# A spectral mixing and SoLU kernel: the twiddle table loaded without gaps and in two parts, x read two chunks at a time, one weight piece converted later

## The chip, the cores and the metric

The kernel runs on one core of a Trainium2 chip. The metric is the time of one launch in microseconds (us), the median of several runs. The profile is one execution recorded by the hardware profiler; its times count from the first instruction. Engines are named as in the profile: PE is the matrix engine (PEld its weight loads), DVE the vector engine, ACT the scalar engine, POOL the GpSimd engine, SP the sync engine, which here does nothing but issue DMAs.

## The reference

```python
def reference(x, w_in, w_out, g_ln):            # x: 8 x 3136 x 256, float32
    X = np.fft.fft(np.fft.fft(x, axis=1), axis=2).real.astype(np.float32)
    t = X.reshape(25088, 256)
    h = t @ w_in                                # w_in: 256 x 1024
    e = np.exp(h - h.max(-1, keepdims=True))
    u = h * e / (e.sum(-1, keepdims=True) + 1e-9)
    u = (u - u.mean(-1, keepdims=True)) / np.sqrt(u.var(-1, keepdims=True) + 1e-6)
    return ((u * g_ln) @ w_out).astype(np.float32)   # w_out: 1024 x 256
```

The weights arrive as 64-bit floats. The kernel sees each of them as two 32-bit words and makes a 32-bit float of them itself.

## The kernel before

The transform over 3136 = 49 x 64 positions is done in two stages. The batch of 8 goes in four pairs. For a pair, 98 partitions hold 2 sequences x 49 values of n1, and the free dimension holds n2 and the 256 features. Since only the real part is wanted, position n2 is first added to its mirror (`add_mirror`, L124) and features d and 256-d are added and subtracted (`fold`, L132). The 32 remaining values of n2 go in eight chunks of four (`CH = 4`, so one chunk of one partition is 4 KB). `load` (L99) fetches a chunk: its own rows go to `xa` over SP's queue, the mirror rows go to `xb` by an indirect DMA that POOL issues. `transform1` (L143) multiplies a chunk by the table `F`, ACT copies the product to `z`, and `keep` (L176) stores it in a scratch tensor `zd` in HBM. `turn` (L179) reads five values of k1 (`KG = 5`) back from `zd` with n2 on the partitions, as `g`. `transform2` (L186) multiplies `g` by the twiddle table `T`, whose rows and columns are split by the two sequences of the pair: the blocks that mix two sequences are zero. `take2` (L198) copies the product to `q`, and `spread` (L202) sends one row of `q` to all partitions as `r`.

The feature transform is folded into the first weight matrix: `product_in` (L448) multiplies the table `Q` by the converted `w_in` and gives `Wi` and `w_mid`. Then come 100 units, one for each pair and each k1 from 0 to 24. A unit makes two blocks of 128 tokens (one if k1 is 0): `up` (L217) on PE, `even` and `join` (L225, L231) on DVE, `expo` on ACT, `product` on DVE with a small mean on POOL, `square` on ACT, `stats` on POOL. The block is then turned: units 0 to 3 by PE transposes (`turn_whole`, L293), all later ones by DVE block transposes and 16 DMAs on SP (`move_blocks`, L310). Four units later (`lag = 4`) `down` (L319) multiplies by `Wo` on PE, `scale` on ACT and `store` finish it. `centre` (L480) subtracts from `Wo` its mean over rows, once.

The order of instructions on each engine is the order in which the code emits them: nothing reorders them. A DMA issue waits on SP like any instruction, and what stands behind it on SP waits too. Semaphores of SP's DMAs are reused in turns of eight, so that an issue also waits until the one eight places earlier has landed.

What matters for the change is the start (L517 to L602), before and during the first units. SP's order is: the first pieces of `w_in` between chunks 0 and 1 of x and `F`; the own rows of chunks 2 and 3; `Q` and `g_ln`; chunks 4 and 5; chunks 6 and 7 and the small stores to `zd`; then, in the middle of chunk 3's step, the two halves of `w_out` (`load_out`) and the table `T` (`load_table`, L437). Chunks 2 to 5 lie in two buffers named `room` that later hold `raw_out` and `uT`. After the eighth chunk, `turn(first, 0, ...)` reads the first `g`, half over SP and half over POOL. The conversion of a weight piece is `exponent`, `confine` and `narrow` (L364 to L405); `narrow` takes the low word by a shift to the right by one and a multiplication by 2^-31. Four pieces of 512 words per partition make `w_in`, four more make `w_out` (`narrow_out(0)` to `narrow_out(3)`, L580 and L585), and all are converted before unit 0 begins. The other four `turn`s of the first pair are issued by POOL in units 0 to 3 (L645).

Of the kernel before, what the change touches and what calls it, by code (L numbers as in the profile page):

```python
# [8 lines left out]

FP32 = mybir.dt.float32  # L10
I32 = mybir.dt.int32
ALU = mybir.AluOpType
ACT = mybir.ActivationFunctionType
AX = mybir.AxisListType
# [20 lines left out]
def kernel(  # L35
# [27 lines left out]
    x_g = x.rearrange("b (n1 g l) d -> (b n1 g) (l d)", n1=N1, l=CH)  # L63
    x_pn = x.rearrange("b (n1 n2) d -> (b n1) n2 d", n2=N2)
    out_k = out.rearrange("(p k2 k1) d -> p k1 k2 d", p=NP, k1=N1)

# [9 lines left out]
    ps_m = ctx.enter_context(tc.tile_pool(name="ps_m", bufs=4, space=PSUM))  # L76

    F = const.tile([PR, 6, ZR], FP32, name="F")
    T = const.tile([P, NK, P], FP32, name="T")
    Wi = const.tile([P, KD, FF], FP32, name="Wi")  # L80
    Wo = const.tile([P, KF, D], FP32, name="Wo")
    ones = const.tile([P, P], FP32, name="ones")
    ident = const.tile([P, P], FP32, name="ident")
    neg_half = const.tile([P, 2], FP32, name="neg_half")
    idx = const.tile([P, NP * (NC + NK - 1)], I32, name="idx")
    w_mid = const.tile([P, FF], FP32, name="w_mid")
    g_ln = const.tile([P, KF], FP32, name="g_ln")
    wbar = const.tile([P, D], FP32, name="wbar")
# [7 lines left out]
            self.raw, self.y, self.y0 = {}, {}, None  # L96
            self.g, self.zs = {}, {}

    def load(pr, c, room=None):  # L99

        r = slice(pr.p * PR, (pr.p + 1) * PR)
        if room is None:
            xa = xpool.tile([PR, CH, D], FP32, tag="xa", name="xa")
            xb = xpool.tile([PR, CH, D], FP32, tag="xb", name="xb")
        else:
            xa, xb = (t.rearrange("p (l d) -> p l d", d=D) for t in room)
# [79 lines left out]
    def transform2(pr, k1):  # L186

        i, k = divmod(k1, KG)  # L190
        g = pr.g[i]
        ps = ps_m.tile([P, KD * P], FP32, tag="m", name="ps2")
        for h in range(KD):
            nc.tensor.matmul(ps[:, h * P : (h + 1) * P], g[:, k, h * P : (h + 1) * P], T[:, k1, :],  # L194
                             start=(h == 0), stop=True, skip_group_check=True)
        return ps

# [163 lines left out]
    def bits(o, i, a, op0, b=None, op1=ALU.bypass):  # L361
        nc.vector.tensor_scalar(out=o, in0=i, scalar1=a, scalar2=b, op0=op0, op1=op1)
# [23 lines left out]
    def narrow(w, raw, outs, unit):  # L386

        if w.dtype == FP32:
            for o, scale in outs:
                nc.vector.tensor_scalar(out=o, in0=o, scalar1=scale, scalar2=2.0 ** 20, op0=ALU.mult, op1=ALU.mult)  # L390
            return
        lo, hi = raw[:, 0 : 2 * NW : 2], raw[:, 1 : 2 * NW : 2]

        bits(mantissa, hi, 0xFFFFF, ALU.bitwise_and, 0x100000, ALU.bitwise_or)
        bits(lo, lo, 1, ALU.logical_shift_right)
        m = lo.bitcast(FP32)
        nc.vector.scalar_tensor_tensor(out=m, in0=lo, scalar=2.0 ** -31, in1=mantissa, op0=ALU.mult, op1=ALU.add)

        nc.vector.scalar_tensor_tensor(out=unit, in0=hi, scalar=top_bit, in1=unit, op0=ALU.bitwise_and,
                                       op1=ALU.bitwise_or)  # L400
        n = NW // len(outs)
        for i, (o, scale) in enumerate(outs):
            r = slice(i * n, (i + 1) * n)
            nc.vector.scalar_tensor_tensor(out=o, in0=m[:, r], scalar=scale, in1=unit[:, r].bitcast(FP32),
                                           op0=ALU.mult, op1=ALU.mult)  # L405

    class Weights:
# [26 lines left out]
            nc.sync.dma_start(out=self.Q, in_=q_tab.rearrange("(c p) d -> p c d", p=P))  # L434
            nc.sync.dma_start(out=g_ln, in_=moe_g_ln.rearrange("(c p) -> p c", p=P))

        def load_table(self):  # L437
            for b in range(2):
                r = slice(b * N2, (b + 1) * N2)
                nc.sync.dma_start(out=T[r, :, r], in_=t_tab)  # L440

        def mid(self):

# [73 lines left out]
    with tc.manual_schedule():  # L517
# [2 lines left out]
        nc.sync.dma_start(out=idx, in_=mirror)  # L520
        make_identity(nc, ident)

        rooms = {}
        for c in range(2, 6, 2):
            room = fpool.tile([P, 2, KF, 4, 64], FP32, tag="uT", name="room", bufs=2)
            room = room[0:PR].rearrange("p w c i m -> p (w c i m)").rearrange("p (a n) -> p a n", a=4)
            rooms[c], rooms[c + 1] = [room[:, i] for i in (0, 1)], [room[:, i] for i in (2, 3)]
        weights.load_in()
        for c in range(4):
            weights.piece_in(c)  # L530
            if c:
                load(first, c - 1, rooms.get(c - 1))
            if c == 1:
                nc.sync.dma_start(out=F, in_=f_tab)
        load(first, 3, rooms[3])
        weights.load_tables()
        for c in range(4, 6):
            load(first, c, rooms[c])
        nc.vector.memset(ones, 1.0)
        nc.vector.memset(neg_half, -0.5)  # L540
        bits(top_bit, neg_half[:, 0:1].bitcast(I32), 31, ALU.logical_shift_right, 31, ALU.logical_shift_left)
# [5 lines left out]
        for c in range(NC):  # L547
# [15 lines left out]
            if c == 3:  # L563
                weights.place_out()
                for i in range(2):
                    weights.load_out(i)
                weights.load_table()
                weights.mid()
                weights.scale_out()
            for s in range(CH // 2):  # L570
                transform1(first, c * CH // 2 + s)
            if c == 3:
                weights.product_in(0)
        turn(first, 0, (nc.sync, nc.gpsimd) * 2)

        confine(weights.units[0], True)
        for i in range(1, 3):
# [3 lines left out]
        weights.exponent_out(3)  # L581
        confine(weights.units[-1])
        weights.product_in(2)
        for i in range(1, 4):
            weights.narrow_out(i)  # L585

        units = [Unit(p, k1) for p in range(NP) for k1 in range(NK)]
# [7 lines left out]
        for i in range(len(units) + lag):  # L595
# [57 lines left out]
def _tables(B, S, D):  # L653
# [30 lines left out]
    mirror = np.zeros((P, B // 2 * (NC + NK - 1)), np.int32)  # L684
    mirror[:PR, : B // 2 * NC] = load.transpose(1, 0, 2).reshape(PR, -1)
    rows = np.arange(B)[:, None, None] * S + (N1 - np.arange(1, NK)) + N1 * np.arange(N2)[::-1, None]
    mirror[:, B // 2 * NC :] = rows.reshape(B // 2, P, NK - 1).transpose(1, 0, 2).reshape(P, -1)
# [39 lines left out]
```

## Time and profile before

| what | value |
|---|---|
| median of 3 runs | 1193.29 us (1191.67 to 1194.35) |
| profiled execution, span of the core | 1189.9 us |
| PE busy | 1154.2 us, 97% of the span |
| DVE busy | 907.9 us, 76% |
| ACT busy | 679.0 us, 57% |
| POOL busy | 496.9 us, 42% |

The span has four parts. Up to about 62 us, x, the tables and the weights come in and the first pair is transformed. From there to about 98 us the first units fill the pipeline. From 98 us to 1172 us the units repeat, and the last 18 us finish the last of them. In the lines that follow, an entry like `58.54 1.99 PE L194 ...` gives the start, the length, the engine, the line, the tiles and the number of instructions, and in square brackets the time the engine stood idle before and what ended that.

### The profile page before, as it was taken

Reading aid. Unit: us, or ns where it says so; the run is one execution under the profiler, and the core shown is the slowest. Engines: PE = TensorE matmul, PEld = TensorE weight load, DVE = VectorE, ACT = ScalarE, POOL = GpSimd, SP = SyncE. Lnnn points to the kernel's source line nnn. Section 1 sums busy time; section 2 is a strip of 40 time slices with the busy share of each in tenths; the row PEclk is TensorE's granted clock in tenths of the full one; section 3 lists DMA queues with packets and bytes.
Section 4 is the critical chain, followed back from the end, with each engine's and each line's share of the span. In section 5 each row is a group of like instructions: output and inputs, shape, how many; then the busy total and the mean of one; then the engine's idle time right before and its main releaser. Section 6 shows DMA issues by size and latency. Waiting matters only on the chain. (4 is left out here: it accounts for less than half of the span.)

```text
span 1189.9 us, 15918 instructions
## 1 busy us (share of the span) xinstructions
PE 1154.2 (97%) x4720; PEld 875.9 (74%) x4720; DVE 907.9 (76%) x1241; ACT 679.0 (57%) x1404; POOL 496.9 (42%) x964
## 2 busy tenths in 40 slices
PE   2889999999999999999999999999999999999998
PEld 1556777777777777777777777777777777777787
DVE  8879777777768877787778878777786887877780
ACT  4557655655546656565555656565555555655561
POOL 3045444443544443432544453433453344333433
PEclk9999999999999999999999999999999999999999
DMA  9873765756775765654775776664684453544534
GB/s 246 206 187 72 190 162 152 200 140 163 171 172 160 187 172 155 167 144 131 172 187 159 176 177 154 158 181 122 150 198 131 109 152 100 145 111 120 142 92 117
DMA packets 460886, 185.39 MB, mean 156 GB/s; under 512 B 428854, under 2 KB 442750, under 8 KB 460800
## 3 DMA queue, kind: packets, MB, share of 16 engines
q1 hardware_dynamic: 446848, 145.63, 48.6%
q0 software_dynamic: 13952, 38.75, 11.9%
q8 instruction: 38, 0.62, 0.2%
q14 instruction: 48, 0.39, 0.1%
HBM read 44.78 MB, written 38.80 MB: 70 GB/s over the span
## 5 line engine op out<-in xcount | busy, mean ns | idle before, releaser
L323 PE MATMUL ps_o<-Wo,uT 128*128 128x256 f32 x3136 | 693.4, 379 | 0.3 <-ACT ot L328 0.3
L323 PEld LDWEIGHTS ps_o<-Wo,uT 128*128 128x128 f32 x3136 | 611.0, 196 | 62.8 <-issue 0.9
L222 PE MATMUL ps_h<-Wi,q 128*128 128x512 f32 x800 | 362.3, 595 | 0.1
L254 DVE SCALAR_TENSOR_TENSOR u<-h,u 128x1024 f32<-128x1024 f32 x196 | 240.1, 1225 | 57.0 <-ACT u L246 31.1
L236 DVE CUSTOM_DVE_ANT_0 h<-ev,ps_h 128x1024 f32<-128x1024 f32 x196 | 231.8, 1219 | 50.3 <-PE ps_h L222 41.3
L256 POOL TENSOR_SCALAR nmean<-usum 128x1 f32<-128x1 f32 x196 | 80.4, 411 | 445.7 <-DVE u L254 445.5
L222 PEld LDWEIGHTS ps_h<-Wi,q 128*128 128x128 f32 x800 | 152.7, 191 | 149.8 <-issue 144.6
L263 ACT ACTIVATE h<-u,nmean 128x1024 f32<-128x1024 f32 x196 | 225.0, 1149 | 61.3 <-POOL nmean L256 60.0
L228 DVE SCALAR_TENSOR_TENSOR ev<-w_mid,r,ps_h 128x1024 f32<-128x1024 f32 x100 | 127.8, 1278 | 133.1 <-PE ps_h L222 126.2
L246 ACT ACTIVATE u<-h,neg 128x1024 f32<-128x1024 f32 x196 | 225.4, 1150 | 6.5
L291 DVE STREAM_TRANSPOSE v<-u 128x1024 f32<-128x1024 f32 x192 | 228.6, 1236 | 0.1
L200 ACT COPY q<-ps 128x256 f32<-128x256 f32 x100 | 37.2, 372 | 289.3 <-PE ps L194 263.0
L328 ACT ACTIVATE ot<-ps_o,rs 128x256 f32<-128x256 f32 x196 | 87.0, 462 | 61.3 <-PE ps_o L323 55.2
L335 POOL DMA_INDIRECT out_dram<-ot,idx x96 | 103.0, 1073 | 35.4 <-issue 20.7
L194 PEld LDWEIGHTS ps<-T,g 128*128 128x128 f32 x400 | 60.9, 194 | 52.1 <-issue 50.9
L169 PE MATMUL ps<-y,F 98*100 98x258 f32 (+3 forms) x288 | 72.2, 387 | 22.2 <-DVE y L122 22.2
L278 POOL TENSOR_TENSOR rs<-v,neg_half 128x2 f32<-128x2 f32 (+1 forms) x100 | 84.2, 842 | 7.8
L244 ACT ACTIVATE neg<-nmax 128x1 f32<-128x1 f32 x196 | 38.3, 195 | 61.0 <-DVE nmax L236 60.2
L169 PEld LDWEIGHTS ps<-y,F 98*100 98x100 f32 x288 | 46.0, 179 | 34.6 <-DVE y L122 20.9
L275 POOL TENSOR_SCALAR v<-ssq 128x2 f32<-128x2 f32 (+1 forms) x100 | 23.3, 233 | 112.7 <-ACT h L263 112.7
L194 PE MATMUL ps<-T,g 128*128 128x128 f32 x400 | 61.5, 277 | 4.4 <-DMA g<-zd 4.4
L184 POOL DMA_DIRECT2D g<-zd x78 | 46.7, 608 | 36.6 <-DMA zd<-z_g 30.5
(74 smaller groups left out, 464.7 us busy)
## 6 DMA issues: line engine op xcount, KB each, us to landing
uT<-v SPq DMA_DIRECT2D x752, 128.0 KB
out_dram<-ot SPq DMA_DIRECT2D x100, 128.0 KB
g<-zd POOLq DMA_DIRECT2D x78, 160.0 KB, 4.2
xa<-in_x_dram SPq DMA_DIRECT2D x28, 392.0 KB
zd<-z SPq DMA_DIRECT2D x24, 400.0 KB
raw_in<-in_moe_w_in_dram SPq DMA_DIRECT2D x4, 512.0 KB
raw_out<-in_moe_w_out_dram SPq DMA_DIRECT2D x2, 1024.0 KB
r<-q SPq DMA_DIRECT2D x100, 0.5 KB
```

The costliest lines, as they stand in the source:

```text
L169: nc.tensor.matmul(o[..., cs], F[:, 2 * t + h, :], i[..., cs], start=first, stop=True, skip_group_check=True)
L194: nc.tensor.matmul(ps[:, h * P : (h + 1) * P], g[:, k, h * P : (h + 1) * P], T[:, k1, :], start=(h == 0), stop=True, skip_group_check=True)
L222: nc.tensor.matmul(ps[:, fs], t.q[:, c * P : (c + 1) * P], Wi[:, c, fs], start=True, stop=True)
L228: nc.vector.scalar_tensor_tensor(out=t.ev, in0=w_mid, scalar=t.r, in1=ps, op0=ALU.mult, op1=ALU.add)
L236: nc.vector.tensor_tensor_reduce(out=t.h[s], in0=t.ev, in1=ps, scale=1.0, scalar=-3.0e38, op0=ALU.subtract if s else ALU.add, op1=ALU.max, ...
L246: nc.scalar.activation(out=t.u[s], in_=t.h[s], func=ACT.Exp, bias=t.neg[:, s : s + 1], accum_out=t.esum[:, s : s + 1])
L254: nc.vector.scalar_tensor_tensor(out=t.u[s], in0=t.h[s], scalar=1.0, in1=t.u[s], op0=ALU.mult, op1=ALU.mult, accum_out=t.usum[:, s : s + 1])
L263: nc.scalar.activation(out=t.h[s], in_=t.u[s], func=ACT.Square, bias=t.nmean[:, s : s + 1], accum_out=t.ssq[:, s : s + 1])
L291: nc.vector.transpose(out=t.batch.v[:, t.w, :, o], in_=t.u[s])
L323: nc.tensor.matmul(ps, uT[:, c, :, s], Wo[:, c, :], start=(c == 0), stop=(c == KF - 1))
L328: nc.scalar.mul(out=t.ot[s], in_=ps, mul=t.rs[:, s : s + 1])
L335: dma = nc.gpsimd.indirect_dma_start(out=out, out_offset=bass.IndirectOffsetOnAxis(ap=idx[:, i : i + 1], axis=0), in_=t.ot[s], in_offset=None)
```

## The change

The diff makes five edits, all of which act in the start or in the first units.

1. `T` is laid out by sequence, then k1, then k2. Each of its blocks is then loaded by one contiguous run for each partition (1280 bytes for the first five k1, 5120 bytes for the other twenty) in place of 25 runs of 256 bytes. Only the first five k1 are loaded with `w_out`; the rest is issued on SP after the first `turn`. The matmul of `transform2` reads `T` in two pieces of 64 columns.
2. `narrow` reads the low word as an unsigned integer and multiplies by 2^-32: the shift goes away.
3. `narrow_out(3)` moves from the start into unit 0, between `expo` and `product`, and `centre` moves from unit 0 to unit 1.
4. Chunks 2 and 3, and chunks 4 and 5, are loaded together by `load_two`: one SP DMA and one indirect DMA for each two chunks, in runs of 8 KB for each partition. `idx` gets four more columns for this.
5. `turn(first, 1)` to `turn(first, 4)` are issued by SP in place of POOL.

```diff
-    T = const.tile([P, NK, P], FP32, name="T")
+    T = const.tile([P, 2, NK, N2], FP32, name="T")
...
+    def load_two(pr, c, room):
+
+        room = room.rearrange("p (a l d) -> p a l d", a=2, d=D)
         r = slice(pr.p * PR, (pr.p + 1) * PR)
+        nc.sync.dma_start(out=room[:, 0], in_=x_pn[r, c * CH + 1 : (c + 2) * CH + 1, :])
+        i = NP * (NC + NK - 1) + c // 2
+        nc.gpsimd.indirect_dma_start(
+            out=room[:, 1].rearrange("p l d -> p (l d)"), out_offset=None, in_=x_g2,
+            in_offset=bass.IndirectOffsetOnAxis(ap=idx[0:PR, i : i + 1], axis=0))
+        pr.raw[c] = (room[:, 0, 0:CH], room[:, 1, CH : 2 * CH], None)
+        pr.raw[c + 1] = (room[:, 0, CH : 2 * CH], room[:, 1, 0:CH], None)
...
-            nc.tensor.matmul(ps[:, h * P : (h + 1) * P], g[:, k, h * P : (h + 1) * P], T[:, k1, :],
+            o = ps[:, h * P : (h + 1) * P].rearrange("p (b k) -> p b k", b=2)
+            nc.tensor.matmul(o, g[:, k, h * P : (h + 1) * P], T[:, :, k1, :],
                              start=(h == 0), stop=True, skip_group_check=True)
...
-        bits(lo, lo, 1, ALU.logical_shift_right)
         m = lo.bitcast(FP32)
-        nc.vector.scalar_tensor_tensor(out=m, in0=lo, scalar=2.0 ** -31, in1=mantissa, op0=ALU.mult, op1=ALU.add)
+        nc.vector.scalar_tensor_tensor(out=m, in0=lo.bitcast(U32), scalar=2.0 ** -32, in1=mantissa, op0=ALU.mult,
+                                       op1=ALU.add)
...
-        def load_table(self):
+        def load_table(self, k1):
             for b in range(2):
-                r = slice(b * N2, (b + 1) * N2)
-                nc.sync.dma_start(out=T[r, :, r], in_=t_tab)
+                nc.sync.dma_start(out=T[b * N2 : (b + 1) * N2, b, k1, :], in_=t_tab[:, k1, :])
...
             weights.piece_in(c)
-            if c:
-                load(first, c - 1, rooms.get(c - 1))
             if c == 1:
+                load(first, 0)
                 nc.sync.dma_start(out=F, in_=f_tab)
-        load(first, 3, rooms[3])
+            elif c == 2:
+                load(first, 1)
+        load_two(first, 2, rooms[0])
         weights.load_tables()
-        for c in range(4, 6):
-            load(first, c, rooms[c])
+        load_two(first, 4, rooms[1])
...
-                weights.load_table()
+                weights.load_table(slice(0, KG))
...
         turn(first, 0, (nc.sync, nc.gpsimd) * 2)
+        weights.load_table(slice(KG, NK))
...
-        for i in range(1, 4):
+        for i in range(1, 3):
             weights.narrow_out(i)
...
                 ps_o = [down(old, s) for s in order]
+            if i == 0:
+
+                weights.narrow_out(3)
             if cur:
                 for s in cur.signs:
                     product(cur, s)
-                if i == 0:
+                if i == 1:
                     weights.centre()
...
             if 0 < i + 1 < NK // KG:
-                turn(first, i + 1)
+                turn(first, i + 1, (nc.sync,) * 4)
```

More of the change, by code (lines that the diff above doesn't have):

```diff
@@ L11 @@
 I32 = mybir.dt.int32
+U32 = mybir.dt.uint32
 ALU = mybir.AluOpType
@@ L63 @@
     x_g = x.rearrange("b (n1 g l) d -> (b n1 g) (l d)", n1=N1, l=CH)
+    x_g2 = x.rearrange("b (n1 g l) d -> (b n1 g) (l d)", n1=N1, l=2 * CH)
     x_pn = x.rearrange("b (n1 n2) d -> (b n1) n2 d", n2=N2)
@@ L84 @@
     neg_half = const.tile([P, 2], FP32, name="neg_half")
-    idx = const.tile([P, NP * (NC + NK - 1)], I32, name="idx")
+    idx = const.tile([P, NP * (NC + NK - 1) + NC // 2], I32, name="idx")
     w_mid = const.tile([P, FF], FP32, name="w_mid")
@@ L97, in __init__, with load @@
             self.g, self.zs = {}, {}
-    def load(pr, c, room=None):
+    def load_two(pr, c, room):
+        room = room.rearrange("p (a l d) -> p a l d", a=2, d=D)
         r = slice(pr.p * PR, (pr.p + 1) * PR)
[L102 to L106, printed above, removed]
+        nc.sync.dma_start(out=room[:, 0], in_=x_pn[r, c * CH + 1 : (c + 2) * CH + 1, :])
[5 more added lines that the diff above has]
+        pr.raw[c + 1] = (room[:, 0, CH : 2 * CH], room[:, 1, 0:CH], None)
+    def load(pr, c):
+        r = slice(pr.p * PR, (pr.p + 1) * PR)
+        xa = xpool.tile([PR, CH, D], FP32, tag="xa", name="xa")
+        xb = xpool.tile([PR, CH, D], FP32, tag="xb", name="xb")
         nc.sync.dma_start(out=xa, in_=x_pn[r, c * CH + 1 : (c + 1) * CH + 1, :])
@@ L521 @@
         make_identity(nc, ident)
[L523 to L527, printed above, removed]
+        rooms = [fpool.tile([P, 2, KF, 4, 64], FP32, tag="uT", name="room", bufs=2) for _ in range(2)]
+        rooms = [room[0:PR].rearrange("p w c i m -> p (w c i m)") for room in rooms]
         weights.load_in()
@@ L683, in _tables @@
     load = row.reshape(-1, PR, 1) * (N2 // CH) + N2 // CH - 1 - np.arange(NC)
-    mirror = np.zeros((P, B // 2 * (NC + NK - 1)), np.int32)
+    two = row[0:2].reshape(PR, 1) * (N2 // CH // 2) + N2 // CH // 2 - 1 - np.arange(NC // 2)
+    mirror = np.zeros((P, B // 2 * (NC + NK - 1) + NC // 2), np.int32)
+    mirror[:PR, B // 2 * (NC + NK - 1) :] = two
     mirror[:PR, : B // 2 * NC] = load.transpose(1, 0, 2).reshape(PR, -1)
     rows = np.arange(B)[:, None, None] * S + (N1 - np.arange(1, NK)) + N1 * np.arange(N2)[::-1, None]
-    mirror[:, B // 2 * NC :] = rows.reshape(B // 2, P, NK - 1).transpose(1, 0, 2).reshape(P, -1)
+    mirror[:, B // 2 * NC : B // 2 * (NC + NK - 1)] = rows.reshape(B // 2, P, NK - 1).transpose(1, 0, 2).reshape(P, -1)
     return {
```

## The prediction

> **What bounds the kernel now.** I read the page first, then the busy time by stretches, then the timelines of PE, SP and DVE over the start.
>
> ```profile
> PE 1154.2 (97%) x4720; PEld 875.9 (74%) x4720; DVE 907.9 (76%) x1241; ACT 679.0 (57%) x1404; POOL 496.9 (42%) x964
> ```
>
> PE is the bound over the whole span. The stretches (columns: length, busy time and instructions of each engine, granted PE clock, DMA share, GB/s) say where it is not:
>
> ```profile
> 0.00:62.00 62.00, 35.37 (x106) 21.31 (x107) 50.54 (x104) 29.45 (x46) 10.73 (x16) 0.97 0.85 217
> 62.00:98.00 36.00, 30.88 (x132) 19.41 (x131) 29.81 (x41) 23.97 (x49) 19.50 (x41) 0.95 0.66 173
> 98.00:1172.00 1074.00, 1073.93 (x4420) 822.70 (x4418) 827.50 (x1097) 623.14 (x1305) 462.75 (x904) 1.00 0.60 153
> 1172.00:1190.00 18.00, 14.06 (x64) 12.47 (x64) 0.00 (x0) 2.40 (x6) 3.90 (x4) 0.96 0.29 93
> ```
>
> From 98 us to 1172 us PE is busy 1073.93 of 1074 us and no edit touches its work there. So the change is worth as many microseconds as it brings that stretch forward. PE's own timeline at the seam (start, length, then idle before and what ended it):
>
> ```profile
> 44.87 2.39 PE L169 MATMUL ps<-y,F 98*100 98x258 f32 x16 [0.39 <-DVE y L122]
> ...
> 50.54 3.60 PE L454 MATMUL wps<-w_in,w_mid 128*128 128x512 f32 x8
> 58.54 1.99 PE L194 MATMUL ps<-T,g 128*128 128x128 f32 x8 [4.40 <-DMA g<-zd]
> 60.32 4.45 PE L222 MATMUL ps_h<-Wi,q 128*128 128x512 f32 x8
> ```
>
> PE has nothing to do for 4.40 us until the first `g` has landed. SP's queue shows why `g` is late:
>
> ```profile
> 36.77 6.12 SPq L440 DMA_DIRECT2D T<-in_t_tab_dram  x2
> 43.00 5.04 SPq L177 DMA_DIRECT2D zd<-z_u  x1
> 48.14 1.63 SPq L177 DMA_DIRECT2D zd<-z_g  x4
> 53.72 0.81 SPq L184 DMA_DIRECT2D g<-zd  x2
> ```
>
> The two issues of `T` take 6.12 us and the next small store 5.04 us, though its data were ready; `zd` of the later chunks follows and `g` waits for all of it. The stretches show what the queue does then, against the 2 KB rows of `w_out` just before:
>
> ```profile
> 38.00:42.00 4.00, 4.00 (x18) 2.75 (x17) 3.95 (x9) 2.40 (x4) 0.00 (x0) 1.00 1.05 401
> 42.00:50.00 8.00, 7.58 (x34) 4.73 (x33) 6.59 (x19) 5.25 (x10) 0.00 (x0) 1.00 1.18 174
> ```
>
> The DMA engines are full in both, at 401 and at 174 GB/s: the second is `T` in 256-byte runs. After PE's wait comes its clock:
>
> ```profile
> 59.00:60.00 1.00, 1.00 (x7) 1.00 (x6) 0.96 (x3) 0.29 (x1) 0.00 (x0) 0.50 0.00 0
> 60.00:61.00 1.00, 1.00 (x4) 0.66 (x4) 0.87 (x2) 0.46 (x2) 0.00 (x0) 0.50 0.00 0
> ...
> 62.00:63.00 1.00, 1.00 (x4) 0.49 (x3) 0.00 (x0) 0.00 (x0) 0.00 (x0) 0.99 0.51 136
> ```
>
> So the first `transform2` and half of the first `up` ran at half clock. On DVE, two lines matter: chunk 4 waits for data, and unit 0's `even` waits for PE, since the weights were ready 2.28 us before.
>
> ```profile
> 34.08 1.22 DVE L129 TENSOR_TENSOR room<-room 98x1020 f32<-98x1020 f32 x1 [2.37 <-DMA room<-in_x_dram]
> ...
> 63.15 1.28 DVE L228 SCALAR_TENSOR_TENSOR ev<-w_mid,r,ps_h 128x1024 f32<-128x1024 f32 x1 [2.28 <-PE ps_h L222]
> ```
>
> **What the Trainium skill says.** "DMA: Bandwidth & Descriptors", Specifications, wants runs of at least 512 B for line rate; the trace agrees (174 against 401 GB/s above). The same page, Queues, rings and completion order, says that a DMA engine takes queues in turn by packets; in the trace 4 KB packets of SP's and POOL's queues pass about one for one from 12 to 24 us, and no packet of 8 KB from x exists yet. "TensorE: Matmul & The Clock Gate", Part 1, says that PE falls to half clock after an idle window of about 3.4 us and needs as long to come back; the clock record has 0.5 from 58.60 to 62.02 us, after 4.40 us of idling.
>
> **The change, part by part.**
>
> *T in long runs, in two parts.* The last copy of chunk 7 to `z_g` ends at 47.30 + 0.59 = 47.89 us on ACT. Before, its store landed at 53.58 (the trace's semaphore records), behind `T`, which landed at 50.94. The first part of `T` is now 2 x 64 runs of 1280 bytes, 164 KB of 819 KB, gone in under 1 us long before 47.89. The store then takes what a small DMA takes on an empty queue: `r` issued at 60.11 landed at 62.13, so 2.0 us, and lands at 49.95. From that landing to the last part of `g` it took 58.34 - 53.58 = 4.76 us, of which two POOL issues of 0.7 us each are part. Against this, the rest of `T` (655 KB, 2.2 us at 300 GB/s) is issued just behind SP's half of `g` and runs beside POOL's half. In turn by packets this costs that half between 0 and 1.7 us; I take 0.85. So `g` is there at 55.55 and PE starts at 55.75 in place of 58.54: 2.8 us gained.
>
> *PE's clock.* PE's earlier products end at 54.14 and the new idle time is 1.6 us, so the clock should stay full. From 58.54 to 63.15 it took 4.61 us to `even`. At full clock a later `transform2` takes 0.61 us for four (L194), the copy to `q` 0.37 us and `up` 0.43 us a matmul: about 1.15 + 4 x 0.43 + 0.2 = 3.1 us, and `r` lands about then too. That gains 1.45 us.
>
> *x in runs of 8 KB.* No bytes are saved. What changes is the wait: chunk 2 now needs chunk 3's data too. In the trace the own rows of chunks 2, 3, 4, 5 landed at 24.06, 27.87, 33.99 and 35.47 us, the mirror rows always before. So at an equal rate chunk 2 starts near 27.9 instead of 26.43, and chunk 4 at 35.5 instead of 34.08: +1.4 us, and all that follows on DVE up to chunk 7 stands in a row behind chunk 4. Whether longer runs go faster the trace doesn't show: 2 KB rows of `w_out` reach 401 GB/s while 4 KB rows of x reach 255 to 285, so run length isn't what holds x back. The bounds are 0 and 2 us (the 3.2 MB of chunks 2 to 5 take 12 us at 270 GB/s; a sixth less is 2 us). I take 0.7, and a loss of 0.7 us in all, which shifts the end of chunk 7 and with it `g`. Longer packets on POOL's queue can also take time from the last pieces of `w_in` (20.70 us), which stand before chunk 1 on DVE; the room for that is 1.4 us, since chunk 2 waits anyway.
>
> *The shift that goes.* Eight instructions at about 0.34 us from start to start (7.61 to 7.95, and so on): 2.7 us of DVE. Those in `w_in` are hidden by the waits for x. Those in `w_out` end before unit 0, where DVE had 2.28 us to spare. Worth nothing by itself.
>
> *`narrow_out(3)` and `centre` later.* Without them DVE would end its weights at 57.80 - 3 x 0.34 = 56.8 and, moved by the 0.7 above, at 57.5, ahead of the new `even` at 63.15 - 2.8 - 1.45 + 0.7 = 59.6. Had `narrow_out(3)` stayed (3.07 - 0.34 = 2.7 us) it would have ended at 60.2 and held `even` by 0.6 us. In unit 0 it fills DVE's wait for the exponential (1.54 us) and pushes `product` by 1.2 us. Behind it on DVE stands unit 1's `even`, which was held before by `centre` (2.3 us, with its wait), so that one starts 1.3 us sooner. `centre` is paid after unit 1's products, and unit 2's `join` comes at the same distance from unit 0's `even` as before (17.5 us), but without the wait of 1.26 us for ACT.
>
> *`turn` on SP.* POOL loses four issues, 2.4 us, in each of units 0 to 3. In unit 1 they had delayed POOL's mean (79.14, with DVE ready at 76.9) and ACT's square waited 2.45 us for it. DVE carries this phase almost without gaps, so I count 0.4 us. On SP the issues now wait for the eight stores to `zd` (73.5 us before), and the next pair's x and unit 3's `r` stand behind; `r` is not needed until 87 us, and `g[1]` at 87.76. Hidden.
>
> *Matmul of T in two pieces.* 400 matmuls at 277 ns, as many columns; L169 reads two strided pieces at the same rate per column as L222. Nothing.
>
> Sum: 2.8 + 1.45 - 0.7 + 0.4 = 3.95 us, so 1193.3 - 3.9 = 1189.4 us.
>
> **The rivals.**
>
> *A. x gains from long runs* (the sixth above, and chunk 4 starts sooner instead of later): the loss of 0.7 turns into a gain of 0.7, 5.3 us in all, 1188.0 us. For it: the DMA share is 0.9 to 1.0 until 36 us, so any rate helps. Against it: the 401 GB/s of 2 KB rows.
>
> *B. The rest of T meets g.* If the collision costs 1.7 us or more, PE's idle time comes near 3.4 us and the clock falls after all: 3.95 - 0.85 - 1.45 = 1.65, and with some luck of the window 2.2: 1191.1 us. For it: POOL's packets of `g` started 2.4 us after the store's landing, just when the rest of `T` will start.
>
> *C. Pairs of chunks come late*: no rate gained, raw `w_in` delayed beyond its room, so 1.9 to 2.7 us lost in place of 0.7: 1191.8 us, hardly to be told from before. For it: the one-for-one turns of the two queues. Against: PE and DVE have waits there to absorb.
>
> *D. Slower*, 1196 us: 8 KB packets of POOL's queue starve `w_in` and `F` by 5 us or more, or SP's longer row of waits holds `r` of an early unit and the fill phase stalls. Against it: SP's slack of 10 us above.
>
> **How the numbers follow.** The forecast (3 to 5 us gained) gets 0.48, A 0.20, B 0.12, C 0.14, D 0.06. Faster by over 0.2% means under 1190.9: forecast, A and a third of B, 0.72. C and the rest of B are within 0.2%: 0.22. D is slower: 0.06. The range goes from A with the full 2 us and a run's scatter (1.2 us below the median before) at 1186.8, to C with scatter at 1192.6, and leaves out D and the edges.
>
> **What would show it.** Right: no 5 us issue on SP near 43 us; the first `transform2` about 56.5 us after under 3 us of idling; PE clock 1.00 through the first `up`; `even` of unit 0 near 59.6; the stretch of steady units as long as before. Chunk 4 starting near 34.8 shows my 0.7; at 35.5 or later C, at 33.5 or sooner A. Wrong at the root: the steady stretch itself longer, or DVE's weights ending after the first `up`.

## The result and the profile after

| kernel | median | against before, same chip |
|---|---|---|
| before | 1192.51 us (1191.67 to 1194.35) | |
| changed | 1199.07 us (1198.69 to 1200.17) | 1.0054, 95% interval [1.0037, 1.0072] |

The change costs 0.54%, 6.4 us. Its profiled execution spans 1196.8 us, 6.9 more than before. The stretches of the changed kernel (length, busy time and instructions of PE, PEld, DVE, ACT, POOL, granted PE clock, DMA share, GB/s):

```profile
0.00:62.00 62.00, 31.66 (x96) 18.65 (x96) 45.22 (x91) 28.79 (x44) 8.48 (x14) 1.00 0.83 217
62.00:98.00 36.00, 31.71 (x119) 18.83 (x120) 28.81 (x43) 20.94 (x44) 13.07 (x23) 0.91 0.80 191
98.00:1172.00 1074.00, 1073.74 (x4427) 822.41 (x4426) 830.82 (x1100) 625.66 (x1310) 459.77 (x906) 1.00 0.70 152
1172.00:1197.00 25.00, 17.69 (x81) 15.20 (x79) 0.00 (x0) 2.84 (x6) 3.89 (x4) 0.92 0.30 87
```

PE is full in the long stretch as before, so the loss lies at the two ends. (The DMA share there rose from 0.60 to 0.70 while PE stayed as busy; the columns of `idx`, below, come back to this.) PE's last matmul ends 3.4 us later than before, at 1189.7 in place of 1186.3 us. But the span after it is longer too: the last store lands at 1191.97 us, and then nothing works, as the last stretches of the changed kernel (same columns) show:

```profile
1188.00:1190.00 2.00, 1.69 (x8) 1.18 (x7) 0.00 (x0) 0.22 (x1) 0.04 (x1) 1.00 0.18 66
1190.00:1192.00 2.00, 0.00 (x0) 0.00 (x0) 0.00 (x0) 0.25 (x1) 0.00 (x0) 1.00 0.18 66
1192.00:1194.00 2.00, 0.00 (x0) 0.00 (x0) 0.00 (x0) 0.00 (x0) 0.00 (x0) 0.76 0.00 0
1194.00:1196.50 2.50, 0.00 (x0) 0.00 (x0) 0.00 (x0) 0.00 (x0) 0.00 (x0) 0.50 0.00 0
```

From 1192 us no engine and no DMA has work. The trace's instruction records name what is still running: an instruction called DRAIN on POOL. It began at 1186.84, took 9.20 us and so ended at 1196.04; POOL's part in the closing barrier of all engines starts at 1196.09, while SP has been ready for it since 1192.5. Before, the DRAIN began at 1183.48 and took 3.46 us, so that it was over before the last store landed and nothing waited for it; the span ended 1.29 us after that landing, and now it ends 4.86 us after. So some 3.6 of the 6.9 us come after the last result has been stored.

At the start, DVE of the changed kernel (start, length, then idle before and what ended it) waits for data at three places:

```profile
25.12 0.43 DVE L374 TENSOR_SCALAR unit<-raw_in 128x512 int32<-128x512 int32 x1 [4.31 <-DMA raw_in<-in_moe_w_in_dram]
31.59 1.22 DVE L140 TENSOR_TENSOR room<-room 98x1020 f32<-98x1020 f32 x1 [1.01 <-DMA room<-in_x_dram]
39.49 1.22 DVE L140 TENSOR_TENSOR room<-room 98x1020 f32<-98x1020 f32 x1 [2.61 <-DMA room<-in_x_dram]
```

The last piece of `w_in` landed at 25.09, before at 20.70, and chunk 4 starts at 39.49, before at 34.08. Not all of this is the change: in the eleven profiles of kernels that load x in single chunks, this one of before included, that piece landed between 20.70 and 22.91 us and chunk 4 started between 33.81 and 37.30. The changed kernel lies outside both ranges. The two profiles add up as follows: chunk 4 starts 5.4 us later; from there to PE's last matmul it takes 2.0 us less (1150.2 in place of 1152.2); and from there to the end 3.6 us more. That makes the 6.9.

On SP the 5 us block behind `T` is gone, and the rest of `T` follows `g`:

```profile
40.71 1.22 SPq L451 DMA_DIRECT2D T<-in_t_tab_dram  x2
42.76 0.31 SPq L188 DMA_DIRECT2D zd<-z_u  x1
46.33 6.84 SPq L188 DMA_DIRECT2D zd<-z_g  x4
54.80 0.80 SPq L195 DMA_DIRECT2D g<-zd  x2
55.66 1.11 SPq L451 DMA_DIRECT2D T<-in_t_tab_dram  x2
```

PE still waits 3.19 us before the first `transform2`, as its timeline in the changed kernel shows (start, length, and the idle time before). By the semaphore records the last part of `g` landed at 62.12 us and the rest of `T` at 62.82, so PE, which started at 62.32, waited for `g` and not for that `T`.

```profile
55.53 3.60 PE L465 MATMUL wps<-w_in,w_mid 128*128 128x512 f32 x8
62.32 1.21 PE L206 MATMUL ps<-T,g 128*128 128x128 f32 x8 [3.19 <-issue]
63.46 5.27 PE L234 MATMUL ps_h<-Wi,q 128*128 128x512 f32 x8
```

Its clock falls here too, from 63.2 to 66.6 us. The stretches of one microsecond show it (the last three numbers are clock, DMA share and GB/s):

```profile
64.00:65.00 1.00, 1.00 (x2) 0.34 (x1) 0.00 (x0) 0.00 (x0) 0.00 (x0) 0.50 0.05 0
65.00:66.00 1.00, 1.00 (x2) 0.34 (x1) 0.00 (x0) 0.00 (x0) 0.00 (x0) 0.50 0.38 95
```

### The profile page after: what moved, and what is told of

The parts are those of the page before. It is cut to its first block, busy times and chain, and to the rows that moved or that the text cites. A ratio compares the mean times of both kernels' runs of the same rounds, so it can differ in the third digit from the quotient of the medians.

```text
span 1196.8 us, 15899 instructions
## 1 busy us (share of the span) xinstructions
PE 1154.8 (96%) x4720; PEld 875.1 (73%) x4720; DVE 904.8 (76%) x1233; ACT 678.2 (57%) x1404; POOL 485.2 (41%) x946
## 4 chain that ended last, share of the span: by engine, by line
PE 92%; DMA 3%; DVE 2%; ACT 1%; issue 1%; POOL 1%; SPq 0%; ACTq 0%; DVEq 0%
PE ps_o L335 57%; PE ps_h L234 28%; PE ps L180 4%; PE ps L206 4%; DMA room<-in_x_dram 2%; DMA xa<-in_x_dram 1%; POOL nmean L268 0%; ACT h L275 0%; DVE u L266 0%; POOL xb L120 0%; DVE y L132 0%; DVE h L248 0%; DVE room L140 0%; ACT unit L395 0%; ACT unit L396 0%
## 5 line engine op out<-in xcount | busy, mean ns | idle before, releaser
L268 POOL TENSOR_SCALAR nmean<-usum 128x1 f32<-128x1 f32 x196 | 83.3, 425 | 453.9 <-DVE u L266 453.7
L212 ACT COPY q<-ps 128x256 f32<-128x256 f32 x100 | 37.1, 371 | 282.5 <-PE ps L206 205.2
L140 POOL TENSOR_TENSOR xa<-xa,xb 98x1020 f32<-98x1020 f32 (+1 forms) x24 | 54.5, 2271 | 0.0
```

## The experiments

Four questions came out of these two traces: do the pairs of 8 KB cost the start (theory S), and if so through POOL's share of the engines (S1) or through the wait for two chunks at once (S2); do the four added columns of `idx`, which move every later buffer by 32 bytes, cost anything (S3 if by alignment, S4 if by mere place; S5 says that the pairs alone cost it all); does the end follow edit 5, which takes 16 DMA issues from POOL (theory U), or something else in the change (W); and does the rest of `T` beside `g` take back what its first part gained (V in the first texts; in that of `edits_123_late_T` this is called S, and X is its rival, that `g` is held by the last copies and stores)? All ratios are against the kernel before on the same chip, as recorded; they can differ from the quotient of the two medians by some 0.1%.

### Taking edit 4 out, doing it alone, and the columns of idx

`after_single` is the changed kernel with the loads of chunks 2 to 5 as before.

```diff
             weights.piece_in(c)
+            if c:
+                load(first, c - 1, rooms.get(c - 1))
...
-        load_two(first, 2, rooms[0])
+        load(first, 3, rooms[3])
...
-        load_two(first, 4, rooms[1])
+        for c in range(4, 6):
+            load(first, c, rooms[c])
```

> The changed kernel with chunks 2 to 5 loaded one by one again as before, and idx at 128 columns; the other four edits stay. Theory S (the pairs of 8 KB are the whole loss: late x at the start, and the four added columns of idx, which move all later buffers by 32 bytes, at the end): the first down comes 5 to 7 us sooner than in the changed kernel, POOL's last DRAIN is back at 3 to 4 us, the DMA share of the steady stretch at 0.60, and the time is 1187 to 1191 us, 0.2% to 0.5% below the kernel before. Rival U (the end comes from POOL having fewer DMA issues, edit 5): the start gains the same, but the DRAIN stays at 9 us and the time is 1191 to 1194. Rival V (the collision of the rest of T with g is the loss): the first down gains less than 2 us and the time stays above 1195.

Measured: 1195.87 us, ratio 1.0034 [1.0018, 1.0050]. Chunk 4 starts at 35.88 us, back in the range of single chunks, and the first `down` comes 4.0 us sooner than in the changed kernel (97.2 against 101.3): S is right about the way at the start, though it said 5 to 7. But the DRAIN stays at 9.28 us, so its second half, that the end comes from `idx`, falls. The time is above before even without the pairs, and above what S and U expected.

`before_pairs` is the kernel before with edit 4 alone.

> The kernel before with edit 4 alone: chunks 2 to 5 in pairs of 8 KB, idx at 132 columns. Theory S: chunk 4 starts 4 to 6 us later than before (about 39.5 us), the first down 5 to 7 us later, POOL's last DRAIN takes 9 us, and the time is 1199 to 1204 us. Rival U: the start loses the same, but the DRAIN stays at 3.5 us, 1196 to 1200. Rival V: within 2 us of the kernel before.

Measured: 1197.89 us, ratio 1.0045 [1.0032, 1.0058]; chunk 4 at 39.79 us; the DRAIN 3.40 us. Edit 4 costs the start, not the end.

`before_idx132` adds only the columns, and `after_idx256` makes `idx` so wide that the buffers behind it lie as before modulo 512 bytes.

```diff
-    idx = const.tile([P, NP * (NC + NK - 1)], I32, name="idx")
+    idx = const.tile([P, NP * (NC + NK - 1) + NC // 2], I32, name="idx")
```

> The kernel before with nothing but four unused columns more in the tile idx, so that every buffer behind it lies 32 bytes further. Theory S (the shift costs the end): the start is unchanged within 0.3 us, the DMA share of the steady stretch rises from 0.60 to 0.70, the 256-byte packets of uT from 16.6 to 21 ns, POOL's last DRAIN from 3.5 to 9 us, and the time is 3 to 4 us above before. Rival U (the shift changes only hidden transfers): share and packets change the same, the DRAIN and the time do not: within 0.1% of before.

> The changed kernel with idx widened to 256 columns, so that the buffers behind it lie as before modulo 512 bytes. Theory S: the start is as late as in the changed kernel (chunk 4 at 39.5 us), the DMA share of the steady stretch is back at 0.60, POOL's last DRAIN at 3.5 us, the time 1194.5 to 1196.5. Rival U: share back at 0.60, but the DRAIN stays at 9 us and the time at 1198 to 1200.

Measured: `before_idx132` 1195.12 us, ratio 1.0021 [1.0012, 1.0029], DRAIN 3.48 us. `after_idx256` 1199.24 us, ratio 1.0056 [1.0042, 1.0070], DRAIN 9.20 us. Both expectations of S for the DRAIN were wrong, and so was U's time for `before_idx132`, within 0.1% of before. The long stretch of `before_idx132` is

```profile
98.00:1172.00 1074.00, 1072.58 (x4415) 821.72 (x4416) 829.45 (x1099) 624.70 (x1308) 461.85 (x906) 1.00 0.71 152
```

so the shift alone gives the DMA share of 0.71 for the same 152 GB/s; 256-byte packets took 21 ns on average there and 17 before. "DMA: Bandwidth & Descriptors", section How a descriptor splits into AXI transactions, in the Trainium skill says that a transaction must start at a multiple of 256 bytes, so that 256 bytes which start elsewhere take two in place of one; the packets agree in sign. The time is another matter: this stretch is PE's, and yet 0.21% was lost. Two more kernels were run for that. `before_idx256` widens `idx` of the kernel before to 256 columns, `before_pairs_idx256` does so with edit 4.

> The kernel before with idx widened to 256 columns, so that every buffer behind it moves by 512 bytes and lies as before modulo 512. Theory S3 (the loss with 132 columns comes from buffers at 32 bytes past a multiple of 256): within 0.1% of before, DMA share 0.60. Rival S4 (it comes from a later place of the buffers whatever the multiple): 0.2% above before, as with 132 columns.

> The kernel before with edit 4 and idx widened to 256 columns. Theory S3 (4.7 us of edit 4 are some 2.2 for the shift by 32 bytes and 2.5 for the pairs): 1195 to 1197 us, 0.15% to 0.3% above before. Rival S5 (the pairs alone cost it all, the shift is nothing where the pairs are): 0.35% to 0.5% above before.

Measured: 1193.14 us, ratio 0.9990 [0.9977, 1.0004], and 1195.41 us, ratio 1.0016 [1.0007, 1.0024]. The stretch of `before_idx256`:

```profile
98.00:1172.00 1074.00, 1072.59 (x4415) 821.79 (x4416) 829.49 (x1099) 624.99 (x1308) 461.74 (x906) 1.00 0.59 152
```

Moving by 512 bytes costs nothing and moving by 32 does, with and without the pairs: S3 holds on the kernel before, where 0.21% and 0.29% (1.0045 against 1.0016) agree. No other shift was tried. In the changed kernel the same alignment brought the DMA share back to 0.59, but no time (1.0056 against 1.0054, each known to about 0.15%). And no single profile shows where the shift's time goes: chunk 4 starts at 36.49 us with it and at 36.98 in the aligned control, and from there to PE's last matmul it takes 1152.3 us with it, 1151.0 in the control and 1152.2 before. So the shift's cost is shown as a ratio on the kernel before; its place, and its share of the 6.4 us, stay open.

Which half of the pairs does it? `before_pool_pairs` pairs only POOL's mirror rows, `before_sp_pairs` only SP's own rows; both have `idx` at 132 columns.

```diff
-        nc.sync.dma_start(out=room[:, 0], in_=x_pn[r, c * CH + 1 : (c + 2) * CH + 1, :])
+        for h in range(2):
+            nc.sync.dma_start(out=room[:, 0, h * CH : (h + 1) * CH],
+                              in_=x_pn[r, (c + h) * CH + 1 : (c + h + 1) * CH + 1, :])
```

> The kernel before with half of edit 4: the mirror rows of chunks 2 to 5 in pairs of 8 KB on POOL, the own rows one by one on SP. Theory S1 (POOL's 8 KB packets get twice the share of the engines and starve SP's w_in and own rows): the last piece of w_in lands 3 to 5 us later than before, chunk 4 starts 3 us later or more, the time is 1195.5 to 1198 us. Rival S2 (the loss is that chunk 2 waits for the own rows of chunk 3): the last piece lands within 1 us of before and the time is within 2.5 us of before, what the wider idx costs.

> The kernel before with the other half of edit 4: the own rows of chunks 2 to 5 in pairs of 8 KB on SP, the mirror rows one by one on POOL. Theory S1: w_in lands no later than before, chunk 2 waits for both own rows (27.9 in place of 26.4 us) and the time is 0 to 2.5 us above before. Rival S2: chunk 2 and chunk 4 start 3 us later or more, the time is 1195.5 to 1198 us.

Measured: 1195.20 us, 1.0023 [1.0014, 1.0032], with the last piece of `w_in` landing at 26.36 us; and 1195.35 us, 1.0013 [1.0002, 1.0023], with that piece at 23.33 us, chunk 2 at 29.62 and chunk 4 at 39.37. With POOL's half alone `w_in` comes late as S1 says; with SP's half alone it comes within 1 us of `before_idx132` (22.40), and chunks 2 and 4 wait for their pair as S2 says. But both times lie just under the 1195.5 us from which S1 and S2 would each have had its half for the cause, and neither ratio stands out of that of the 32 bytes which both kernels carry (1.0021). So each mechanism is seen in its trace, and in the time only both together are (1.0045, or 1.0016 where aligned).

### Edit 5 and the end

`edits_123` is the kernel before with edits 1 to 3, `before_sp_turns` the kernel before with edit 5 alone.

```diff
-                turn(first, i + 1)
+                turn(first, i + 1, (nc.sync,) * 4)
```

> The kernel before with edits 1, 2 and 3: chunks loaded one by one, and the turns of units 0 to 3 issued by POOL as before. Theory U (POOL's last DRAIN takes 9.3 us in place of 3.4 because POOL has 16 DMA issues fewer): the DRAIN is back at 3.4 us, the span ends 1 us after the last landing in place of 4.9, and the time is 1190.5 to 1192.5 us, 3.3 us below the kernel with edit 5. Rival W (the DRAIN follows from T's layout or the late weight piece): it stays at 9.3 us and the time at 1195 to 1196.

> The kernel before with edit 5 alone: the turns of units 0 to 3 issued by SP. Theory U: POOL's last DRAIN takes 9.3 us, the start gains 0 to 0.6 us, and the time is 1195.5 to 1197.5 us. Rival W: the DRAIN stays at 3.4 us and the time is within 0.6 us of before.

Measured: `edits_123` 1193.28 us, ratio 1.0011 [1.0003, 1.0019], DRAIN 3.46 us; `before_sp_turns` 1197.19 us, ratio 1.0040 [1.0025, 1.0055], DRAIN 9.28 us. W falls: edit 5 alone makes the DRAIN long, and without it the DRAIN is short. The time of `edits_123` is above what U expected; the next part deals with that. To see whether it is the number of issues or these issues, `after_single_half_turns` leaves every second DMA of the turns on POOL, and `single_pool_r` leaves the turns on SP but lets POOL issue eight other, small DMAs far from both ends:

```diff
-        nc.sync.dma_start(out=t.r, in_=t.q[0:1, P : 2 * P])
+        (nc.gpsimd if t.p == 2 and 8 <= t.k1 < 16 else nc.sync).dma_start(out=t.r, in_=t.q[0:1, P : 2 * P])
```

> As the changed kernel with single chunks, but only half of the turns of units 0 to 3 on SP, the other half on POOL: 8 POOL issues more. If the DRAIN jumps at some number of POOL issues, it is 3.4 or 9.3 us; if it grows with each missing issue, it is 6.3 us. Time 1192 to 1196 us accordingly. Rival W: 9.3 us.

> As the changed kernel with single chunks (turns of the first pair on SP), but the rows r of 8 units in the middle of the run are spread by POOL in place of SP: 206 DMA issues of POOL in all, the number that the kernel with half of the turns had. Theory U (the number of POOL's DMA issues decides its last DRAIN): 3.2 to 3.5 us in place of 9.3, and the time 1192 to 1193 us. Rival (the turns of the first pair themselves, by their place or their size, decide it): 9.3 us and 1195.5 to 1196.5.

Measured: 1192.90 us, 1.0003 [0.9993, 1.0012], DRAIN 3.20 us; and 1192.48 us, 0.9986 [0.9976, 0.9997], DRAIN 3.16 us. Eight DMA issues more on POOL bring the end back, as parts of the turns in the first units as well as small rows in mid-run. So U holds, and it is a jump, not a slope. Over all profiles:

```
POOL's DMA issues   last DRAIN          last landing to end of span
196 and 198         9.20 to 9.28 us     4.86 to 4.96 us     (4 profiles)
206 to 214          3.16 to 3.48 us     0.92 to 1.29 us     (13 profiles)
```

What POOL does in those 6 us the trace doesn't show, so the cause behind the number stays open; nor was a number between 198 and 206, below 196 or above 214, tried.

### The rest of T, and the turns

`edits_123_late_T` moves the rest of `T` from behind the first `turn` into unit 0.

```diff
         turn(first, 0, (nc.sync, nc.gpsimd) * 2)
-        weights.load_table(slice(KG, NK))
...
+            if i == 0:
+                weights.load_table(slice(KG, NK))
             if 0 < i + 1 < NK // KG:
                 turn(first, i + 1)
```

> Edits 1, 2 and 3, with the rest of T issued in unit 0 in place of right behind the first g. Theory S (the rest of T takes g's bandwidth): g lands 1.5 to 3 us sooner than with the rest beside it, PE idles under 1 us before the first transform2, its clock stays at 1.00 through the first up, the even of unit 0 comes 3 to 4.5 us sooner, and the time is 1187 to 1189.5 us. Rival X (g is held by the last copies and stores of z_g, not by T): the even of unit 0 moves by less than 1 us and the time is within 1 us of edits 1, 2 and 3.

Measured: 1190.93 us, ratio 0.9984 [0.9976, 0.9992], 0.27% better than `edits_123` against the same runs of before. That is below the kernel before, though above what S expected. PE of `edits_123` waits at the seam (first two lines), and PE of this kernel hardly does (last three):

```profile
58.51 1.13 PE L196 MATMUL ps<-T,g 128*128 128x128 f32 x8 [3.31 <-DMA T<-in_t_tab_dram]
59.66 3.70 PE L224 MATMUL ps_h<-Wi,q 128*128 128x512 f32 x8
...
53.12 3.60 PE L455 MATMUL wps<-w_in,w_mid 128*128 128x512 f32 x8
57.09 1.13 PE L196 MATMUL ps<-T,g 128*128 128x128 f32 x8 [0.37 <-ACT unit L385]
58.97 3.70 PE L224 MATMUL ps_h<-Wi,q 128*128 128x512 f32 x8 [0.76 <-ACT q L202]
```

The eight matmuls of `up` take 3.70 us in both, where the changed kernel's took 5.27: the clock fell in neither, so the gain here is not the clock. From the landing of the last `z_g` store to the last part of `g`, by the trace's semaphore records, it is 52.29 to 56.89, 4.60 us; with the rest of `T` beside it (`edits_123`) 50.78 to 58.31, 7.53 us. The profile names `T` as what ended PE's wait of 3.31 us, but the rest of `T` landed at 59.08, after PE had started; the last part of `g`, at 58.31, ended it. So X falls: the collision costs 2.9 us. What is gained is then partly lost in unit 1. ACT's square of that unit

```profile
79.40 1.15 ACT L265 ACTIVATE h<-u,nmean 128x1024 f32<-128x1024 f32 x1 [5.75 <-POOL nmean L258]
```

waits 5.75 us for a mean of two small instructions, and POOL shows why they are late:

```profile
73.00 2.38 POOL L185 DMA_DIRECT2D g<-zd  x4 [2.41 <-DMA xa<-in_x_dram]
75.69 2.10 POOL L110 DMA_INDIRECT xb<-in_x_dram,idx  x1 [0.30 <-issue]
78.09 0.96 POOL L110 DMA_INDIRECT xb<-in_x_dram,idx  x1 [0.30 <-issue]
79.08 0.45 POOL L258 TENSOR_SCALAR nmean<-usum 128x1 f32<-128x1 f32 x2
```

The turn cannot be issued before the eight big stores to `zd` have landed (72.46 us, the last of them, in the semaphore records), and the means stand behind it. So the means wait until the stores are through, however early unit 0 starts. This is the wait that edit 5 takes away. `edits_123_spread_turns` therefore has, besides the late rest of `T`, the second turn on SP, and the others only when they are needed, on POOL in units 4, 7 and 11; `spread_turns_sp` has them all on SP and the eight `r` of above on POOL.

```diff
+        TURNS = {0: (1, (nc.sync,) * 4), 4: (2,), 7: (3,), 11: (4,)}
...
-            if 0 < i + 1 < NK // KG:
-                turn(first, i + 1)
+            if i == 0:
+                weights.load_table(slice(KG, NK))
+            if i in TURNS:
+                turn(first, *TURNS[i])
```

> Edits 1, 2 and 3 with the rest of T in unit 0, the second turn of the first pair on SP, and the third to fifth on POOL in units 4, 7 and 11 in place of 1, 2 and 3; 210 DMA issues of POOL. Theory (what the late T gained at the start was lost again in units 1 to 3, where POOL's turns and the indirect loads hold its mean back and four turns at once fill the DMA engines): ACT's wait for the mean of unit 1 falls from 5.75 us to under 2, PE's clock stays at 1.00 from 70 to 98 us, the DRAIN is 3.5 us, and the time is 1186.5 to 1189.5 us. Rival (the mean is held by the indirect loads alone, or the later turns hold the steady units): 1190 to 1192 us.

> Edits 1, 2 and 3 with the rest of T in unit 0 and all turns of the first pair on SP, in units 0, 4, 7 and 11; the rows r of 8 units in the middle spread by POOL, so that POOL has 206 DMA issues. Theory (POOL's issue in unit 4 held a product of DVE and its own mean in the version with spread turns): the square of unit 5 does not wait 2.2 us for the mean, and the time is 1187.5 to 1189.5 us. Rival (PE is the bound again from unit 5): within 0.1% of the version with spread turns, 1189 to 1191.

Measured: 1189.58 us, ratio 0.9970 [0.9962, 0.9979], DRAIN 3.31 us; and 1188.62 us, ratio 0.9963 [0.9948, 0.9977], DRAIN 3.16 us. The intervals of the two overlap, so the rival of the second text, no difference between them, is not excluded. In `spread_turns_sp` the wait of 5.75 us has become

```profile
72.17 1.15 ACT L265 ACTIVATE h<-u,nmean 128x1024 f32<-128x1024 f32 x1 [1.11 <-POOL nmean L258]
74.36 1.15 ACT L265 ACTIVATE h<-u,nmean 128x1024 f32<-128x1024 f32 x1 [0.95 <-POOL nmean L258]
```

In `edits_123_spread_turns` it is 1.11 and 0.95 us too. But the clock, which was expected to stay full there up to 98 us, is at half from 95.55 us for 3.41 us. Both beat the kernel before by 3.6 to 4.4 us (1193.3 times 0.0030 and 0.0037) with edits 1, 2 and 3, the turns of edit 5 in part or later, and nothing of edit 4.

How much of this comes from the turns is not shown. Since chunk 4 starts at a different time in each profile, the times in the following table, in us, are counted from there:

| from the start of chunk 4 to | before | `edits_123` | `edits_123_late_T` | `edits_123_spread_turns` | `spread_turns_sp` |
|---|---|---|---|---|---|
| `even` of unit 0 | 29.1 | 26.5 | 24.0 | 24.0 | 24.7 |
| mean of unit 1 | 45.1 | 44.5 | 42.0 | 37.1 | 37.8 |
| `even` of unit 6 | 80.4 | 80.1 | 77.4 | 77.2 | 77.7 |
| PE's last matmul | 1152.2 | 1152.3 | 1148.6 | 1148.5 | 1149.5 |

`edits_123` is 2.6 us ahead of the kernel before at the `even` of unit 0, 0.6 at the mean of unit 1, and nothing is left at the end. With the late `T` 3.7 us are left. With the turns spread, the mean comes 4 to 5 us sooner still, and yet unit 6 and the end come no sooner: PE waits in later units instead (2.02 us before 84.28 and again before 93.17 us in `spread_turns_sp`). Against `edits_123_late_T` the two ratios are better by 0.14% and 0.21%, on other chips, with intervals that just touch.

## Why the prediction was wrong, step by step

The forecast was 1189.4 us, a gain of 3.95; the time was 1199.07, a loss of 6.4. Edit by edit, with the ratios of the chain before, `edits_123`, `after_single`, changed kernel times 1193 us. By the intervals the three steps are good to about 1, 2 and 3 us, and the last of them is not clear of noise:

| step | forecast | measured | miss |
|---|---|---|---|
| edits 1 to 3 | -2.8 - 1.45 | +1.3 | 5.6 |
| edit 5 | -0.4 | +2.7 | 3.1 |
| edit 4 | +0.7 | +2.4 | 1.7 |

Four steps of the prediction failed. The collision of the rest of `T` with `g`, taken at 0.85 us, cost 2.9. The path was followed to the `even` of unit 0 only, and what was gained there was lost again behind it, 2.6 us ahead becoming nothing. The end of the program, put at nothing, cost 3.6 us after edit 5. And the pairs of chunks, taken at 0.7 us, cost about 2. The rest of this section takes them term by term.

*Where the bound lies* was right: the steady stretch stayed PE's, and the 5 us issue on SP near 43 us went away.

*T in long runs.* The term that failed is "In turn by packets this costs that half between 0 and 1.7 us; I take 0.85". The collision of the rest of `T` with POOL's half of `g` cost 2.9 us (7.53 against 4.60). The other term, 4.76 us from the store's landing to `g`, was right: 4.60 where nothing collides. From chunk 4 to the `even` of unit 0, two points of one profile, the kernel before takes 29.06 us, `edits_123` 26.49 and `edits_123_late_T` 23.98. So the collision left 2.6 of a gain of 5.1, and my 2.8 + 0.85 + 1.45 = 5.1 without it was the right size (4.4 to 5.1 in the three kernels with the late `T`).

*PE's clock.* "The clock should stay full" failed in the changed kernel, after 3.19 us of idling, for the reason that rival B gave. It is not a matter of the length of the gap alone: the clock fell after 2.35 us in `after_single`, whose `up` then took 5.26 us, and did not after 3.31 us in `edits_123`, whose `up` took 3.70:

```profile
57.85 1.21 PE L196 MATMUL ps<-T,g 128*128 128x128 f32 x8 [2.35 <-ACT w_mid L456]
59.00 5.26 PE L224 MATMUL ps_h<-Wi,q 128*128 128x512 f32 x8
```

"TensorE: Matmul & The Clock Gate", Part 1, in the Trainium skill says that the window in which PE's activity is judged runs freely; the trace agrees in so far as a gap's place decides as well as its length. But a whole idle window of about 3.4 us, on which the forecast counted, was not needed: 2.35 us were enough. A term that counts on a full clock should have kept both cases.

*narrow_out(3) and centre.* That the weights would be ready before `even` was right (DVE has been waiting for PE again, 6.65 us in the changed kernel). What I didn't see is where the gain goes next. I followed the path to the `even` of unit 0 and took that for the whole; the stores to `zd`, issued after it, and POOL's turn behind them set a second point, the mean of unit 1. Counted from chunk 4 it came 45.1 us later before and 44.5 in `edits_123`, so of the 2.6 us gained at the `even` 0.6 were left. From the `even` of unit 0 to that of unit 6, `edits_123` takes 53.62 us and the kernel before 51.38. This stage scatters, though: `after_single` and `single_pool_r`, which are the same there, took 51.43 and 54.35. In part this is PE's clock: between these two points the record has 6.83 us at half clock in `edits_123` and `single_pool_r`, and 3.41 in before and `after_single`.

*turn on SP.* "Hidden" failed, and at a place that the forecast never looked at: the end. With 16 issues fewer POOL's DRAIN took 9.3 in place of 3.4 us, and the span ended some 3.6 us later. In the fill the edit may have been worth more than my 0.4: with the DRAIN short again, turns on SP gave 0.9986 (`single_pool_r`) and on POOL 1.0011 (`edits_123`), 0.25% or 3.0 us, but on two chips. On the kernel before no such gain shows: 0.40%, 4.8 us, is no less than the DRAIN's part. So this stays open.

*x in runs of 8 KB.* "I take 0.7" is a term too small: 1.9 us on the aligned kernel before (0.16%, interval 0.07% to 0.24%), and 2.4 us in the changed kernel, which by itself is within its noise. "The room for that is 1.4 us" did not hold, since the last piece of `w_in` came 4.4 us later than in the profile of before and 2.2 later than in any with single chunks. The mechanism is what rival D named first, in part: from 14 to 20 us of the changed kernel 118 packets of 8 KB of POOL's queue and 119 of 4 KB of SP's started, one for one, and took 552 and 272 ns each, so that POOL's queue got two thirds of the bytes. SP's own pairs add the wait for two chunks. Nothing was gained in rate: 274 GB/s from 4 to 24 us, before 286, and 248 to 286 over all kernels. Chunk 4 at 39.49 us was far past the 35.5 that I had laid out as the sign of rival C.

*The columns of idx* were not priced at all. On the kernel before they cost 0.21%; in the changed kernel that is not shown.

Rival D had the sign right, at 1196 us, and its first half names what edit 4 did. That its number came within 3 us of the time is luck: edit 4 cost about 2 us of the 6.4, and the collision, the loss behind unit 0 and the end are not in it. I gave it 0.06 because of "SP's slack of 10 us", which speaks only to its second half. Rival C's 1191.8 does not follow from its own terms: with 1.9 to 2.7 us lost in place of 0.7 the sum is 1190.5 to 1191.4, so C lay across the edge between faster and the same.

## What to carry to other kernels

A table that is cut in two so that its first part comes early must also have its second part where the queues are empty: right behind the critical load, it cost 2.9 us here, about half of what the cut had gained. After shortening one path, follow the next two or three waits behind it on every engine, since a transfer that was issued off the path can be the next bound. Before moving DMA issues from one engine to another, look at how each engine ends, not only at the place they are moved from; and when runs are made longer on one of two queues, count in bytes what each queue gets for a packet. And before a single profile is read against another, ask how much its start scatters: here count from a common point, such as chunk 4.

## What the runs showed that was not expected

- POOL's last DRAIN takes 3.16 to 3.48 us with 206 to 214 DMA issues of POOL in the program and 9.20 to 9.28 us with 196 or 198; eight DMAs of 512 bytes in mid-run are enough to go from the long one to the short one.
- Moving all buffers by 32 bytes made the 256-byte transfers of the steady stretch fill 0.71 in place of 0.60 of the DMA engines' time at the same 152 GB/s, and cost 0.21% of a kernel that PE bounds; moving them by 512 bytes did neither.
- The start of the same code differs: the kernels that load x in single chunks share their first loads, and yet chunk 4 began anywhere between 33.81 and 37.30 us. The profile of before, at 34.08, was an early one, so single profiles of the start can't be compared to better than some 2 us.
- PE's clock fell to half after an idle time of 2.35 us and did not after one of 3.31.
